# A pair's queries, keys and decays in three transfers at three places of the SyncE queue, instead of one

## The chip, the cores and the metric

One core of a Trainium2 chip runs the whole program. The metric is the device time of one execution in microseconds. Smaller is better.

## What is computed

A linear-attention layer with a decaying state is followed by two gated layers. The reference, cut down:

```python
# r, k, v, w: (4, 8, 768, 48); u: (8, 48)
for t in range(768):
    cur = einsum('bhd,bhe->bhde', u * k[t], v[t])
    y[t] = einsum('bhd,bhde->bhe', r[t], state + cur)
    state = w[t][..., None] * state + einsum('bhd,bhe->bhde', k[t], v[t])
x = y as (3072, 384)
x = (sigmoid(x @ w_gate) * (x @ w_val)) @ w_out          # 384 -> 1536 -> 384
h = x @ w_in                                             # 384 -> 2048
out = (h * tanh(softplus(h))) @ w_out2                   # 2048 -> 384
```

## The kernel before

**Stages.** Time is cut into 24 chunks of 32 steps, and two chunks make a *pair* (12 pairs, NP). For a pair, the queries, keys and decays (r, k, w, called R, K and W in the code) of 32 rows lie in one tile `blk` of 128 partitions and 10,240 bytes each; there are two such tiles, `blk[p % 2]`. For pair p the kernel does:

- `load_pair(p)`: fill `blk`. Pair 0 comes in three transfers (R, K, W), all others in one of 1,280 KB.
- `fine(p)`: GpSimd (POOL) multiplies queries by keys into `pt` tiles and folds decays into R, K and W in place (`update`, L455 for all of them); VectorE (DVE) sums each `pt` into the matrix `A` (L476). The first two products need R and K alone; every `update` of R or K needs W too.
- `coarse(p)` and `keys(p)`: DVE transposes K, R, W and A into `KD`, `RD`, `WD` and `X` (L566, L560, L573, L611); TensorE (PE) multiplies them (`lp`, L595); POOL and DVE scale them; K is updated twice more and transposed into `KT` (L654). That last transpose frees `blk[p % 2]` for pair p+2.
- `step(j)`, twice: outputs `yp` (L680), then the state `s` is decayed (L756), key-value products `kp` (L783) are made and added (`join`, L794). The outputs are split into two fp16 halves (`xs`, L207) and transposed by a DMA from the ScalarE queue into `xt` (L714).
- `gate(p, f)`, f from 0 to 11: 18 matmuls for gate and value (L828), then ScalarE and DVE make `gt`. `out1(p, c, part)`: output sums of the first gated layer (L892), three column groups c of four parts; after the fourth, `xo` is made and **stored to HBM** in `x2d` (L928).
- The second gated layer (L1013, L1058) follows at the end and reads `x2d` back.

`v` comes in its own transfers (`load_v`, four of 96 KB for a chunk), weights in raw tiles of 768 KB that are decoded on the chip.

**Order.** The program adds tasks with costs and dependences to a `Plan`; `Plan.run` computes due times backwards and lets each engine take the ready task with the earliest due time. What comes out is a fixed instruction order for each engine, in which the chip then runs it. All loads and stores named above are issued by SyncE (SP), one after another: an issue that waits holds all behind it. In the main loop over p (L1180), `gate(p, f)` and `out1(p-1, ...)` are added for f = 0 to 11, `tail1(p+1)` (coarse, keys and first step of the next pair) at f = 4, and `tail2(p+1)` (second step, `load_pair(p+3)`) and `fine(p+2)` at f = 7. On PE one turn of this loop, called *turn p* here, is 24 groups of nine gate matmuls, 12 groups of nine output sums, and between them, from f = 4 on, the many small matmuls of `lp`, `yp` and `kp`. From the last step's `kp` of a turn to f = 4 of the next there are none of these.

```python
        keys = [("blk", p % 2, i) for i in range(3)]
        if p:
            attn("sp", 3.6, lambda e: go(e, None), [], keys, lat=2.0)
```

Of the kernel before, what the change touches and what calls it, by code (L numbers as in the profile page):

```python
# [25 lines left out]
KC = DM // 128  # L26
# [29 lines left out]
class Plan:  # L56
# [11 lines left out]
    def add(self, eng, cost, fn, reads=(), writes=(), lat=SEM, burst=False):  # L68
        t = Task()
        t.cost = eng if isinstance(eng, dict) else {eng: cost}  # L70
        t.fn, t.lat, t.burst = fn, lat, burst
        t.rank = len(self.tasks)
        t.deps = set()
        for k in reads:
            if k in self.writer:
                t.deps.add(self.writer[k])
        for k in writes:
            if k in self.writer:
                t.deps.add(self.writer[k])
            t.deps.update(self.readers.pop(k, ()))  # L80
        for k in reads:
            self.readers.setdefault(k, []).append(t)
        for k in writes:
            self.writer[k] = t
        self.tasks.append(t)
# [66 lines left out]
def mixer_moe_kernel(  # L152
# [32 lines left out]
    x2d = dram.tile([NP, KC, 128, 2, NT], F16, name="x2d")  # L185
# [11 lines left out]
    def attn(eng, cost, fn, reads=(), writes=(), lat=SEM, burst=False):  # L197
        add(eng, cost, fn, [*reads, "attention"], writes, lat, burst)

    def split(key, src, hi, lo, scale, cost, reads, new):  # L200

        def high(e):
            new()
            nc.scalar.activation(out=hi(), in_=src(), func=AF.Copy, scale=scale)

        def rest(e):
            nc.vector.scalar_tensor_tensor(  # L207
                out=lo(), in0=src(), scalar=scale, in1=hi(), op0=ALU.mult, op1=ALU.subtract
            )

        add("act", cost, high, reads, [(*key, 0)])
        add("dve", cost, rest, [*reads, (*key, 0)], [(*key, 1)])
# [185 lines left out]
    kd = {}  # L398
    wd = {}
    lps = {}  # L400
    yps = {}
    kps = {}
    xss = {}
# [10 lines left out]
    def load_pair(p):  # L414
        edges = (0, C * DH, C * (DH + DP), BLK)

        def new(e):
            blk[p] = fp.tile([128, BLK], F32, tag=f"blk{p % 2}", name=f"blk{p}")

        def go(e, i):  # L420
            if i is None:
                new(e)
            cs = slice(0, BLK) if i is None else slice(edges[i], edges[i + 1])
            nc.sync.dma_start(out=blk[p][:, cs], in_=rkw[p, :, cs])

        keys = [("blk", p % 2, i) for i in range(3)]
        if p:
            attn("sp", 3.6, lambda e: go(e, None), [], keys, lat=2.0)
        else:
            attn("none", 0, new, [], keys, lat=0.0)  # L430
            for i in range(3):
                attn("sp", 1.2, lambda e, i=i: go(e, i), [], [keys[i]], lat=2.0)

    def load_v(j):
        def go(e):
# [444 lines left out]
    def out1(p, c, part):  # L880
        last = p == NP - 1
        bank = "po2" if last and c == 1 else "po"
        cs = slice(128 * c, 128 * c + 128)
        fr = range(3 * part, 3 * part + 3)

        def sums(e):
            if part == 0:
                pool = w2["po"] if bank == "po2" else po
                ops[p, c] = pool.tile([128, 512], F32, tag="po", name=f"o1{p}_{c}")
            for f in fr:  # L890
                for n, (a, g) in enumerate(((0, 0), (1, 0), (0, 1))):
                    nc.tensor.matmul(  # L892
                        ops[p, c][:, :NT],
                        wos[:, a, f, cs],
                        gt[p][:, g, f, :],
                        start=(f == 0 and n == 0),
                        stop=(f == NF1 - 1 and n == 2),
                    )

        reads = [("gt", p % 2, f, a) for f in fr for a in range(2)]  # L900
        reads.append(("gt", p % 2, "tile"))
        reads += [("wo", f // 2, a) for f in fr for a in range(2)]
        if bank == "po2":
            reads.append("open")
        add("pe", 0.99, sums, [*reads, "outs"], [bank])
        if part < 3:
            return
        n = nxo[0]
        nxo[0] += 1
        xo = ("xo", n % 3)  # L910

        def new():
            xos[n] = mp.tile([128, 2, NT], F16, tag=f"xo{n % 3}", name="xo")

        split(
            xo,
            lambda: ops[p, c][:, :NT],
            lambda: xos[n][:, 0],
            lambda: xos[n][:, 1],
            SX / (SW * SG),  # L920
            0.35,
            [bank],
            new,
        )
        add(
            "sp",
            0.4,
            lambda e: nc.sync.dma_start(out=x2d[p, c], in_=xos[n]),  # L928
            [(*xo, 0), (*xo, 1)],
            [("x2d", p, c)],  # L930
            lat=2.0,
        )
# [43 lines left out]
    def load_x2(r):  # L976
        def go(e):
            x2[r] = w2["p"].tile([128, 2, KC, NR], F16, tag=f"x2{r % 2}", name=f"x2_{r}")
            for i in range(2):
                for h in range(2):  # L980
                    nc.sync.dma_start(
                        out=x2[r][:, h, :, NT * i : NT * i + NT],
                        in_=x2d[2 * r + i, :, :, h].rearrange("c p n -> p c n"),
                    )

        src = [("x2d", 2 * r + i, c) for i in range(2) for c in range(KC)]
        add("sp", 2.4, go, [*src, "open"], [("x2", r % 2)], lat=2.0)
# [139 lines left out]
    attn("pool", 0.4, unit, [], ["eye"])  # L1127
    attn("sp", 0.1, lambda e: nc.sync.dma_start(out=U, in_=ub), [], ["U"], lat=2.0)
    load_pair(0)
    load_pair(1)  # L1130
    for j in range(3):
        load_v(j)
# [13 lines left out]
    def tail1(p):  # L1146
        coarse(p, cells[p])
        keys(p)
        step(2 * p)

    def tail2(p):
        step(2 * p + 1)
        if p + 2 < NP:
            load_pair(p + 2)

    def tail_end():
        done = [("blk", i, n) for i in range(2) for n in range(3)]
        done += [("pt", i) for i in range(5)] + [("A", i) for i in range(8)] + ["A"]
        add("none", 0, open_a, [], [*done, "opened"])
        for i in range(8):  # L1160
            cs = slice(256 * i, 256 * i + 256)
            dst = lambda cs=cs: w2["wi"][:, :, :, cs]
            load_raw(("wi", i), lambda: dp, in_cols(wi, cs), (KC, 256), i % 3)
            decode(("wi", i), dst, (KC, 256), i, i % 3, ["opened"], W2HI, W2LO)
        add("none", 0, open_b, [], ["attention", "open"])
        for i in range(8):
            cs = slice(2 * i, 2 * i + 2)
            dst = lambda cs=cs: w2["wp"][:, :, cs]
            slot = (i + 2) % (3 + NRAW)
            pool = (lambda: dp) if slot < 3 else (lambda: w2["raw"])  # L1170
            reads = [] if slot < 3 else ["open"]
            load_raw(("wp", i), pool, in_rows(wo2, cs), (2, DM), slot, reads)
            decode(("wp", i), dst, (2, DM), i, slot, ["open"], W2HI, W2LO)
# [6 lines left out]
    for p in range(NP):  # L1180
        for f in range(NF1):
            if p + 1 < NP:
                if f == YPOS[0]:
                    tail1(p + 1)
                if f == YPOS[1]:
                    tail2(p + 1)
                    if p + 2 < NP:
                        cells[p + 2] = fine(p + 2)
                    else:
                        tail_end()  # L1190
            if f == 0 and p >= NP - 1:
                load_x2(0)
                load_x2(1)
            gate(p, f)
            if p > 0:
                out1(p - 1, f // 4, f % 4)
    add("none", 0, lambda e: None, [], ["gates", "free_g"])
    add(
        "act",
# [61 lines left out]
```

## Time and profile before

| | |
|---|---|
| runs | 1020.68, 1025.45 and 1024.71 us; median 1024.71 us |
| profiled execution | 1025.36 us; its span, first to last instruction, 1023.6 us |
| busy share of the span | PE 92%, DVE 50%, ScalarE 34%, POOL 30% |
| mean granted TensorE clock | 0.988 of full speed |
| HBM traffic | 56.64 MB read, 9.44 MB written |

The profile names for each stretch in which an engine stands idle what ended it: another engine's instruction, a DMA, or "issue", if the engine waited for nothing that the profile shows. `PEld` are the weight loads of the PE, which overlap its matmuls. Queue q1 carries the DMAs that SP issues, q10 those of ScalarE, and q8 the instructions. Times within the trace are in microseconds from the first instruction.

### The profile page before, as it was taken

The page shows a single profiled execution, that of the slowest core. Times are in us where ns is not written, and L with a number is a line of the kernel's source. Part 1 is how long each engine was busy: PE and PEld are TensorE (multiplying, and loading weights), DVE is VectorE, ACT ScalarE, POOL GpSimd, SP SyncE. Part 2 cuts the span into 40 slices and gives each one's busy share as a digit, 9 for nine tenths or more (in the row PEclk, how much of TensorE's full clock was granted, in tenths as well). Part 3 has the DMA queues.
Part 4 walks back from the last instruction along what each step waited for, and adds up shares of the span by engine and source line. Part 5 has one row for each costly group of instructions (what it writes and reads, how often), then busy time and mean ns, then how long its engine had stood idle before and what let it go on. Part 6 is the DMA issues. An engine that isn't in the chain of part 4 may idle for free.

```text
span 1023.6 us, 32777 instructions
## 1 busy us (share of the span) xinstructions
PE 941.2 (92%) x14952; PEld 678.8 (66%) x14952; DVE 512.9 (50%) x831; ACT 347.1 (34%) x693; POOL 307.6 (30%) x322
## 2 busy tenths in 40 slices
PE   0388789989999899989999999999999999999998
PEld 0266678868878687878888887655555555555555
DVE  5899988866666556666658557221111111111110
ACT  3347622212212122222226356433333333333320
POOL 8873589671744444454113011000000000000000
PEclk9999899989999899999999999999999999999999
DMA  9345543222140404040206351010100101000000
GB/s 303 125 168 177 198 95 110 45 100 91 33 91 29 90 28 90 29 100 20 60 9 173 107 175 42 11 37 16 41 14 16 39 16 47 9 16 16 8 16 31
DMA packets 53595, 72.12 MB, mean 70 GB/s; under 512 B 20432, under 2 KB 37328, under 8 KB 52048
## 3 DMA queue, kind: packets, MB, share of 16 engines
q1 hardware_dynamic: 36816, 66.09, 21.2%
q10 hardware_dynamic: 16640, 3.94, 2.4%
q8 instruction: 117, 1.92, 0.8%
q14 instruction: 22, 0.18, 0.1%
HBM read 56.64 MB, written 9.44 MB: 65 GB/s over the span
## 4 chain that ended last, share of the span: by engine, by line
PE 78%; DVE 9%; DMA 4%; issue 3%; POOL 2%; ACT 2%; ACTq 0%; SPq 0%; DVEq 0%
PE gv L828 22%; PE o L1058 18%; PE h L1013 18%; PE o L892 11%; PE yp L680 3%; PE kp L783 3%; PE lp L595 3%; DMA raw_wo<-wo 1%; POOL pt L455 1%; DVE A L476 1%; POOL blk L455 1%; DVE word_wi L286 1%; DMA raw_wp<-wo 1%; DMA raw_wv<-wv 1%; DVE X L611 1%
## 5 line engine op out<-in xcount | busy, mean ns | idle before, releaser
L1013 PE MATMUL h<-x,wis 128*128 128x512 f16 x864 | 201.5, 379 | 0.0
L828 PE MATMUL gv<-xt,wgs 128*128 128x256 f16 x1296 | 167.4, 277 | 11.7 <-DVE gt L859 5.7
L828 PE MATMUL gv<-xt,wvs 128*128 128x256 f16 x1296 | 168.1, 276 | 4.3 <-issue 4.3
L892 PE MATMUL o<-gt,wos 128*128 128x256 f16 x1296 | 167.5, 275 | 4.4 <-DVE xo L207 1.9
L455 POOL TENSOR_TENSOR blk<-blk 128x384 f32<-128x384 f32 (+1 forms) x144 | 125.9, 890 | 70.0 <-DVE KD L566 59.3
L828 PEld LDWEIGHTS <-wgs 128*128 128x128 f16 x1296 | 124.9, 99 | 30.5 <-issue 12.6
L1013 PEld LDWEIGHTS <-wis 128*128 128x128 f16 x864 | 84.5, 98 | 90.7
L892 PEld LDWEIGHTS <-wos 128*128 128x128 f16 x1296 | 127.2, 98 | 24.2 <-issue 4.8
L828 PEld LDWEIGHTS <-wvs 128*128 128x128 f16 x1296 | 121.9, 99 | 23.4 <-issue 4.6
L839 ACT ACTIVATE sig<-gv 128x256 f32<-128x256 f32 x144 | 55.0, 383 | 236.4 <-PE gv L828 225.2
L1024 ACT ACTIVATE e<-h 128x512 f32<-128x512 f32 x96 | 57.3, 597 | 207.5 <-PE h L1013 207.5
L455 POOL TENSOR_TENSOR pt<-blk 128x384 f32<-128x384 f32 (+1 forms) x96 | 108.4, 1154 | 51.4 <-DMA blk<-rkw 47.3
L844 DVE SCALAR_TENSOR_TENSOR gv<-gv,sig 128x256 f32<-128x256 f32 x144 | 61.7, 429 | 82.7 <-ACT sig L839 82.2
L856 ACT CAST gt<-gv 128x256 f16<-128x256 f32 x144 | 53.2, 371 | 76.1 <-DVE gv L844 69.1
L859 DVE TENSOR_TENSOR gt<-gv,gt 128x256 f16<-128x256 f32 x144 | 60.3, 419 | 32.2 <-ACT gt L856 32.1
L595 PE MATMUL lp<-RD,KD 64*16 64x16 f32 (+1 forms) x3072 | 34.5, 185 | 37.0 <-DVE RD L560 33.6
L1031 DVE SCALAR_TENSOR_TENSOR wos<-e,wos 128x512 f16<-128x512 f32 x27 | 18.7, 692 | 84.5 <-ACT wos L1027 84.5
L595 PEld LDWEIGHTS lp<-RD,KD 64*16 64x16 f32 (+1 forms) x3072 | 29.8, 101 | 46.1 <-DVE RD L560 33.6
L1058 PE MATMUL o<-wps,wgs 128*128 128x384 f16 x324 | 58.5, 326 | 0.0
L1058 PE MATMUL o<-wps,wos 128*128 128x384 f16 x324 | 57.2, 326 | 0.0
L1031 DVE SCALAR_TENSOR_TENSOR wgs<-e,wgs 128x512 f16<-128x512 f32 x27 | 18.7, 692 | 73.8 <-ACT wgs L1027 73.8
L783 PE MATMUL kp<-v,KT 32*32 32x48 f32 x2944 | 45.9, 212 | 8.6 <-issue 7.5
(92 smaller groups left out, 1051.0 us busy)
## 6 DMA issues: line engine op xcount, KB each, us to landing
blk<-rkw SPq DMA_DIRECT2D x11, 1280.0 KB, 6.7
v<-vt SPq DMA_DIRECT2D x96, 96.0 KB, 3.3
raw_wi<-wi SPq DMA_DIRECT2D x8, 768.0 KB, 4.9
raw_wp<-wo SPq DMA_DIRECT2D x8, 768.0 KB, 4.4
raw_wg<-wg SPq DMA_DIRECT2D x6, 768.0 KB, 4.5
raw_wv<-wv SPq DMA_DIRECT2D x6, 768.0 KB, 4.8
raw_wo<-wo SPq DMA_DIRECT2D x6, 768.0 KB, 4.4
x2d<-xo SPq DMA_DIRECT2D x36, 128.0 KB, 1.8
```

Source lines behind the costliest of these rows:

```text
L455: engines[e].tensor_tensor(out=pv, in0=a, in1=b, op=ALU.mult)
L595: nc.tensor.matmul(out, kd[p][gs, x, :m], rhs, start=True, stop=True, skip_group_check=True)
L783: nc.tensor.matmul(kps[j, hf][o : o + 32, i, :], KT[o : o + 32, p % 2, HG * e + x, :], vs[j][o : o + 32, x, :], start=True, stop=True,)
L828: nc.tensor.matmul(gps[p, f][:, o], w[:, a, kc, fs], xt[p][:, c, kc, :], start=(n == 0), stop=(n == 3 * KC - 1),)
L839: nc.scalar.activation(out=sgs[p, f], in_=gps[p, f][:, 0], func=AF.Sigmoid, scale=1.0 / (SW * SX))
L844: nc.vector.scalar_tensor_tensor(out=gps[p, f][:, 1], in0=gps[p, f][:, 1], scalar=SG / (SW * SX), in1=sgs.pop((p, f)), op0=ALU.mult, op1=A ...
L856: nc.scalar.copy(out=gt[p][:, 0, f], in_=gps[p, f][:, 1])
L859: nc.vector.tensor_tensor(out=gt[p][:, 1, f], in0=gps[p, f][:, 1], in1=gt[p][:, 0, f], op=ALU.subtract,)
L892: nc.tensor.matmul(ops[p, c][:, :NT], wos[:, a, f, cs], gt[p][:, g, f, :], start=(f == 0 and n == 0), stop=(f == NF1 - 1 and n == 2),)
L1013: nc.tensor.matmul(hps[r, f], w2["wi"][:, a, kc, fs], x2[r][:, c, kc, :], start=(n == 0), stop=(n == 3 * KC - 1),)
L1024: nc.scalar.activation(out=es[r, f], in_=hps[r, f], func=AF.Mish, scale=ih)
L1058: nc.tensor.matmul(ops2[r, t][:, :DM], g2[r][f][:, c, tsl], w2["wp"][:, a, f, :], start=(f == 0 and n == 0), stop=(f == NF2 - 1 and n == 2),)
```

## The change

Pair 1 is still loaded at once. All other pairs are loaded in three transfers: R (384 KB), K (512 KB), W (384 KB). For pairs 2 and 3 the three are added together, where the one was. From pair 4 on only R is added there; K is added after the output sums of turn p-3, f = 11, with a planner's dependence on the store of `x2d[p-4]`, group 2, and W in turn p-2 after f = 3, with one on the store of `x2d[p-3]`, group 0. These dependences only set the order in the SP queue; the chip waits in front of them because the store, which waits for `xo`, is issued first.

```diff
         keys = [("blk", p % 2, i) for i in range(3)]
-        if p:
+        if p == 1:
             attn("sp", 3.6, lambda e: go(e, None), [], keys, lat=2.0)
-        else:
-            attn("none", 0, new, [], keys, lat=0.0)
-            for i in range(3):
-                attn("sp", 1.2, lambda e, i=i: go(e, i), [], [keys[i]], lat=2.0)
+            return
+
+        after = [[], [("x2d", p - 4, KC - 1)], [("x2d", p - 3, 0)]]
+        attn("none", 0, new, [], keys, lat=0.0)
+        for i in range(3):
+            late[p, i] = lambda i=i: attn(
+                "sp", 1.2, lambda e: go(e, i), after[i] if p > 3 else [], [keys[i]], lat=2.0
+            )
+            if p <= 3 or i == 0:
+                late.pop((p, i))()
...
+            if f == 3 and p > 1 and (p + 2, 2) in late:
+                late.pop((p + 2, 2))()
+            if f == 11 and (p + 3, 1) in late:
+                late.pop((p + 3, 1))()
```

The whole plan is made anew with it, so the order moves on every engine. On SP, one turn in the middle of the loop. Before, with the stores of `x2d[3]` group 0, 1, 2 and `x2d[4]` group 0 around the load of pair 8:

```order
L928 DMA x2d_86<-xo_4525 128x512
L424 DMA blk8_4932<-rkw 128x2560
L440 DMA v13_5032<-vt 32x768 x4
L928 DMA x2d_86<-xo_4905 128x512
L440 DMA v14_5235<-vt 32x768 x4
L928 DMA x2d_86<-xo_5265 128x512
L928 DMA x2d_86<-xo_5408 128x512
```

Now, with the stores of `x2d[3]` group 1 and 2 and of `x2d[4]` group 0 and 1:

```order
L935 DMA x2d_86<-xo_4868 128x512
L447 DMA v13_4949<-vt 32x768 x4
L447 DMA v14_5197<-vt 32x768 x4
L425 DMA blk8_5214<-rkw 128x768
L935 DMA x2d_86<-xo_5226 128x512
L425 DMA blk7_4342<-rkw 128x1024
L935 DMA x2d_86<-xo_5360 128x512
L425 DMA blk7_4342<-rkw 128x768
L935 DMA x2d_86<-xo_5753 128x512
```

The load of a pair no longer stands between the stores of group 0 and group 1; R of one pair and K of the pair before it stand around the store of group 2, and W stands behind the store of group 0.

On DVE, in the second half of turn 7 (`kp16_1` is the PE's last key product of chunk 16, `s17` the state that it is added to, which `yp17` needs). Before:

```order
L654 STREAM_TRANSPOSE KT_92<-blk9_5815 128x24x32
L207 SCALAR_TENSOR_TENSOR xs16_7566<-yp16_7461,xs16_7566 128x384
L207 SCALAR_TENSOR_TENSOR xo_7554<-o16_1_7226,xo_7554 128x256
L859 TENSOR_TENSOR gt7_7087<-gv7_7_7447,gt7_7087 128x256
L794 TENSOR_TENSOR s17_6876<-kp16_1_7588,s17_6876 128x384
L756 TENSOR_TENSOR s18_7568<-s17_6876,WD8_5878 128x384
```

Now:

```order
L207 SCALAR_TENSOR_TENSOR xo_7523<-o16_1_7184,xo_7523 128x256
L483 TENSOR_REDUCE A_91<-pt_7474 128x2x4x4
L207 SCALAR_TENSOR_TENSOR xs16_7538<-yp16_7431,xs16_7538 128x384
L618 STREAM_TRANSPOSE X9_7556<-A_91 128x32x32
L801 TENSOR_TENSOR s17_6843<-kp16_1_7561,s17_6843 128x384
L573 STREAM_TRANSPOSE KD9_7623<-blk9_6112 128x32x32
L851 SCALAR_TENSOR_TENSOR gv7_8_7528<-gv7_8_7528,sig_7621 128x256
L567 STREAM_TRANSPOSE RD9_7679<-blk9_6112 128x32x32
```

The last sum into A for pair 9 and the transposes into X, KD and RD now stand together around that join; before, the X transpose that stood next was one of pair 10, later in the turn.

## Rows read from the trace of the kernel before

**Rows 1.** The page: busy time of each engine, and the queue of instructions (packets, MB, share).

```profile
PE 941.2 (92%) x14952; PEld 678.8 (66%) x14952; DVE 512.9 (50%) x831; ACT 347.1 (34%) x693; POOL 307.6 (30%) x322
...
q8 instruction: 117, 1.92, 0.8%
```

**Rows 2.** Waits of PE from 145 to 600 us: total us, times, longest.

```profile
PE gv L828 <- issue: 8.6, 2, 4.3
PE yp L680 <- issue: 3.8, 2, 2.7
PE o L892 <- issue: 1.8, 1, 1.8
...
PE gv L828 <- DVE gt L859: 1.3, 1, 1.3
PE kp L783 <- issue: 0.8, 2, 0.4
```

**Rows 3.** Busy time by stretch: length, engines (instructions), granted clock, DMA share, GB/s.

```profile
163.03:460.53 297.50, 281.50 (x6555) 238.44 (x6552) 192.67 (x322) 67.55 (x176) 155.34 (x163) 0.98 0.28 69
310.76:363.55 52.79, 48.52 (x1095) 40.59 (x1093) 29.77 (x52) 10.98 (x29) 22.57 (x25) 0.94 0.26 56
460.53:506.26 45.73, 45.73 (x1094) 39.15 (x1092) 29.49 (x52) 10.99 (x29) 13.72 (x17) 1.00 0.16 38
```

**Rows 4.** Timeline in turn 5: start, length, engine, line, what, idle before it.

```profile
340.86 0.34 SPq L424 DMA_DIRECT2D blk<-rkw  x1
...
353.31 1.86 PE L828 MATMUL gv<-xt,wgs 128*128 128x256 f16 x8 [4.27 <-issue]
```

**Rows 5.** DMA from 341 to 350 us: queues (packets, MB, share), issue (KB, landing).

```profile
q1 hardware_dynamic: 242, 1.53, 75.9%
q10 hardware_dynamic: 805, 0.20, 20.1%
...
blk<-rkw SPq DMA_DIRECT2D x1, 1280.0 KB, 7.7
```

**Rows 6.** DMA from 350 to 353 us: the queue of instructions.

```profile
q8 instruction: 1, 0.02, 2.9%
```

**Rows 7.** Busy time by stretch, right behind that wait of PE.

```profile
353.30:359.00 5.70, 5.69 (x84) 4.04 (x84) 0.00 (x0) 0.00 (x0) 3.00 (x4) 0.50 0.07 14
```

**Rows 8.** Busy time by stretch: one without small matmuls, one with many.

```profile
316.00:321.00 5.00, 5.00 (x48) 4.49 (x46) 2.53 (x5) 1.33 (x4) 3.83 (x5) 1.00 0.00 0
...
331.00:336.00 5.00, 5.00 (x162) 4.34 (x148) 4.15 (x5) 0.65 (x2) 0.86 (x1) 1.00 0.03 7
```

**Rows 9.** Timeline of SP: stores of output sums, groups 2 and 0, in turn 6.

```profile
364.61 11.15 SPq L928 DMA_DIRECT2D x2d<-xo  x2
```

**Rows 10.** Instructions that write v, from 490 to 500 us: durations ns, first and last start.

```profile
L440 SPq DMA_DIRECT2D v<-vt x4: 332/416/1391, 492.9 to 495.2; - x4
```

**Rows 11.** Busy time by stretch, while that v lands.

```profile
495.00:500.00 5.00, 5.00 (x160) 4.33 (x152) 2.92 (x5) 1.62 (x4) 0.00 (x0) 1.00 0.21 63
```

**Rows 12.** Groups of instructions by form: count, busy us, mean ns, idle before.

```profile
L611 DVE STREAM_TRANSPOSE X<-A 128x1024 f32<-128x1024 f32 x12 | 23.4, 1953 | 0.0
...
L794 DVE TENSOR_TENSOR s<-kp,s 128x384 f32<-128x384 f32 x44 | 23.9, 547 | 14.7 <-PE kp L783 14.1
```

**Rows 13.** Waits of PE from 60 to 163 us.

```profile
PE gv L828 <- DVE gt L859: 4.5, 3, 2.4
PE kp L783 <- issue: 2.9, 2, 1.5
```

**Rows 14.** Timeline of SP: the load of pair 4.

```profile
132.20 0.35 SPq L424 DMA_DIRECT2D blk<-rkw  x1
```

**Rows 15.** Waits of POOL, whole span: total us, times, longest.

```profile
POOL pt L455 <- DMA blk<-rkw: 47.3, 9, 11.5
```

**Rows 16.** DMA issues, whole span: count, KB each, median us to landing.

```profile
blk<-rkw SPq DMA_DIRECT2D x11, 1280.0 KB, 6.7
...
blk<-rkw SPq DMA_DIRECT2D x2, 384.0 KB, 4.1
```

More of the change, by code (lines that the diff above doesn't have):

```diff
@@ L400, in mixer_moe_kernel @@
     lps = {}
+    late = {}
     yps = {}
```

## The prediction

> **What bounds the kernel now.** I read the page first. PE is busy for 92% of the span [rows 1], and turn 8 has no idle PE at all [rows 3], so only what stops PE counts. Next came PE's waits. From 145 to 600 us other engines cause little; 15.0 us (8.6 + 3.8 + 1.8 + 0.8) are put down to "issue" [rows 2]: PE had what it needs and nothing to run. Third, the time by turns. Turn 8, with about the same matmuls, takes 45.73 us, turn 5 takes 52.79 [rows 3]. What differs is the load of a pair: turn 5 has one, turn 8 none (pair 11 was loaded before).
>
> Fourth, what happens around one such wait. In turn 5 SP issues the load of 1,280 KB at 340.86; PE stands for 4.27 us and goes on at 353.31 [rows 4]. From 341 to 350 us the window's DMA answer lists two queues alone, q1 and q10, together 96% of the 16 engines; there is no packet of q8, the queue of instructions [rows 5]. From 350 to 353 there is one [rows 6]. PE and PEld run 2 x 14952 instructions and q8 brings 117 packets of some 16 KB [rows 1], so a packet holds about 256 of them if nearly all are PE's. Where the small matmuls are, PE starts 162 + 148 = 310 instructions in 5 us, without them 48 + 46 = 94 [rows 8]. So a late packet hurts only among the small matmuls: 256 instructions are 4.1 us there (256 / 310 x 5) and 13.6 us elsewhere. I read the wait as: **PE's next instructions come late because the long load of a pair fills the DMA engines in the dense half of a turn.** [...]
>
> **The change part by part.** *Where the transfers go.* In the new SP order, R of one pair stands behind both v of the turn, the second of which waits for the turn's last `kp`; then the store of group 2, then K. All that lies in the stretch with 94 instructions in 5 us, where 13.6 us go by for each 256. W stands behind the store of group 0. The two stores' issues run from 364.61 to 375.76 [rows 9], and turn 6 begins at 363.55 [rows 3], so W is issued about 12.2 us into the turn, where `lp` begins, and it is 384 KB.
>
> *Gain.* Turns 2 to 7 take 297.50 us [rows 3]. At turn 8's pace they take 6 x 45.73 = 274.4, which is 23.1 less. The other way to count: issue waits 15.0, and a clock of 0.98 over 297.5 us [rows 3], 6 us; together 21. Loads from pair 5 on and most of pair 4's leave the dense halves, so I take the middle: **-22 us**, with 15 (waits alone) and 23.1 as ends.
>
> *W among the small matmuls.* Its own price is not shown. Upper end: the smaller of the two issue waits of `yp`, 3.8 - 2.7 = 1.1 us [rows 2], for each of pairs 4 to 11: 8.8 us. Lower end 0: a v, four transfers of 96 KB and so the same 384 KB, is issued from 492.9 to 495.2 [rows 10] in the dense half, and PE is busy for all of the next 5.00 us with 160 matmuls [rows 11]. That is the nearest row, so I take **0**.
>
> *Two more issues and two more landings for a pair.* An issue holds SP for 0.34 us [rows 4]; SP has 11 us between stores [rows 9]. A transfer of 384 KB lands after 4.1 us where the whole lands after 6.7 [rows 16], so the parts take longer in sum. Who waits is POOL: it already waits 47.3 us in nine waits for pairs to land [rows 15], and PE doesn't wait for it in these turns [rows 2]. The cover is that a pair is loaded about two turns before its `lp`. The change spends most of it: W comes in turn p-2 at 12 us, and `lp` follows at the same place of turn p-1, 46 us later. POOL's work for a turn (13.7 to 22.6 us) and DVE's (about 30) [rows 3] must fit in there. **0**; without cover see the rivals.
>
> *The state's join.* POOL's products now end in the middle of the turn, so DVE's X transpose (1.95 us) stands directly before the join of `kp` to the state (0.55 us) [rows 12], for which `yp` waits. Between that `kp` and `yp` PE has 18 gate matmuls, 1.9 us at 48 in 5 us [rows 8]. If the transpose starts just as `kp` ends, PE waits 1.95 + 0.55 - 1.9 = 0.6 us; if it starts earlier, not at all. Ends 0 and, with the whole transpose late, 1.95 us in each of eight turns, 15.6. The natural place is between 0 and 0.6: 0.25 x 8 = **+2 us**.
>
> *The start.* Up to turn 1 DVE and the weights decide, and the plan has other orders there. PE's wait for issue before `kp`, 1.5 us at most [rows 13], falls beside the load of pair 4 at 132.20 [rows 14], whose K and W now come later: **-1.5**. PE's 4.5 us of waits for `gt` [rows 13] may go or come twice: ends -4.5 and +4.5.
>
> *The end.* Pair 11 is finished later, its W being held back into turn 9, and with it begins the decoding of the second layer's weights, still some turn and a half before its first matmul. That burst costs 1.3 us in a wait for `gt` [rows 2]; it may be paid twice. **+0.5**, ends 0 and 1.3.
>
> **Sum**: -22 + 0 + 0 + 2 - 1.5 + 0.5 = -21. The profiled execution took 1025.36 us: 1.76 outside its span of 1023.6, which the change leaves alone. 1025.36 - 21 = 1004.4. It lies 0.65 above the median of the runs shown, within their spread of 4.8.
>
> **The rivals.** *Chain too short, slower.* W is now late by plan, and all of a pair's POOL and DVE work hangs on it, in order: products, A, X, the join, `yp`. Each microsecond that the last product is later than I count makes `yp` wait one microsecond in eight turns. At 21 / 8 = 2.6 us a turn the gain is gone. [...] For it: W lands about when POOL needs it. Against: PE never waits for POOL there now, and POOL has half of each turn free. [...] 5%.
>
> *A late packet has another cause, no change.* If the instruction queue takes turns with the others, a packet waits for one packet of data and not for a load, and cutting the load leaves the waits where they are: the gain term is 0, and 1025.36 + 2 - 1.5 + 0.5 = 1026. For it: loads of one size go with waits from 0.4 to 4.3 us [rows 2]. Against: no packet of q8 in 9 us beside two full queues [rows 5]. [...] 6%.
>
> *Half.* W, or the heap of v, R, store and K (384 + 384 + 128 + 512 = 1,408 KB, more than the old load) that spills past its sparse stretch, still starves PE: 1.1 to 2.7 us [rows 2] a turn, 9 to 22 us of eight turns given back without the clock, so 1013 to 1026, likeliest 1014. 10%.
>
> **How the numbers follow.** Forecast 79%, half 10%, no change 6%, slower 5%. The forecast's own ends: 1025.36 - 23.1 - 4.5 = 998 with nothing lost, and 1025.36 - 15 + 1 = 1011 with the waits alone. To leave no more than 2 in 10 out the range goes on to the likely part of "half": 998 to 1015. About 0.5% (5 us) is what a measurement of this kernel can tell from no change: faster than 1019.6 takes the forecast and most of "half", 88%; within it 7%; slower 5%.
>
> **What would show it.** Right: issue waits of PE between 145 and 550 us under 3 us in all; no stretch at 0.50 of the clock there; turns 2 to 7 at 45.7 to 46.5 us each; in a turn's dense half only W and one v. The join term: waits of `yp` for DVE's `s`, under 0.6 us each. Wrong: issue waits just behind W's issue; PE waiting for X or `s` for microseconds; turns over 48 us; or a new slow-clock stretch in the first 160 us, which the new order there could cause as well as remove.

## The result, and the profile after

The changed kernel takes **1007.54 us** (median of four runs, 1006.19 to 1010.17), the kernel before in the same session 1022.69 (four runs, 1018.63 to 1025.45): a ratio of 0.9856, 95% interval 0.982 to 0.9891. Forecast were 1004.4, between 998 and 1015. The profiled execution of after took 1010.17 us with a span of 1008.4; it is the slowest of the four. Line numbers of after are 7 higher than before's from `load_v` on (`gv` L835, `lp` L602, `yp` L687, `kp` L790).

The page of after: PE's busy time, the granted clock in 40 slices, the queue of instructions. They answer to [rows 1].

```profile
PE 937.8 (93%) x14952; PEld 678.7 (67%) x14952; DVE 521.2 (52%) x830; ACT 345.9 (34%) x692; POOL 309.8 (31%) x324
...
PEclk9998889999999999999999999999999999999999
...
q8 instruction: 117, 1.92, 0.8%
```

The same instructions come in the same 117 packets, and PE is busy 3.4 us less. So the span, 15.2 us shorter, shrank mostly in PE's idle time. PE's waits in after from 145 to 600 us (total us, times, longest), to be laid beside [rows 2]:

```profile
PE o L899 <- DVE xo L207: 2.4, 2, 1.7
PE yp L687 <- DVE X L625: 1.3, 1, 1.3
PE yp L687 <- DVE s L801: 0.5, 1, 0.5
PE gv L835 <- DMA xt<-xs: 0.2, 1, 0.2
```

The word "issue", under which 15.0 us stood, is gone. The instruction packets come in time: in turn 5, from 30.2 to 39.2 us behind its start, before has none [rows 5], and after, in the same part of the turn (335.2 to 344.2 us), has two:

```profile
q8 instruction: 2, 0.03, 1.3%
```

Time by stretch in after (length, busy time of PE, PEld, DVE, ScalarE, POOL, clock, DMA share, GB/s): turn 0, turn 1, turns 2 to 8, and turn 10.

```profile
60.64:115.89 55.25, 44.02 (x1022) 35.44 (x1015) 48.99 (x88) 35.86 (x70) 25.17 (x25) 0.85 0.60 190
115.89:167.64 51.75, 45.90 (x1077) 39.75 (x1074) 46.33 (x69) 20.44 (x42) 35.33 (x35) 0.93 0.40 99
167.64:488.07 320.43, 320.40 (x7646) 274.14 (x7644) 215.23 (x360) 76.20 (x203) 156.01 (x167) 1.00 0.26 68
...
533.81:581.84 48.03, 44.55 (x966) 37.92 (x964) 36.40 (x53) 24.98 (x47) 16.24 (x9) 1.00 0.46 134
```

The same view of before, for the same turns:

```profile
60.92:109.90 48.98, 40.37 (x1138) 33.05 (x1134) 45.84 (x86) 33.34 (x67) 25.03 (x25) 0.97 0.61 198
109.90:163.03 53.13, 46.05 (x962) 38.38 (x956) 45.97 (x69) 20.77 (x41) 42.12 (x41) 0.94 0.47 124
163.03:506.26 343.23, 327.23 (x7646) 277.59 (x7644) 222.17 (x373) 78.54 (x205) 169.06 (x179) 0.98 0.26 64
553.46:598.29 44.83, 44.22 (x964) 37.79 (x965) 26.61 (x46) 18.80 (x41) 6.30 (x4) 1.00 0.35 108
```

In after PE is busy for 320.40 of the 320.43 us of turns 2 to 8, at full clock: seven turns of 45.73 to 45.93 us, turn 8's pace of before [rows 3] in each. Before took 343.23 for the same 7,646 matmuls. The balance of the two profiled executions: turns 2 to 8 **-22.8 us**; turns 0 and 1 together 107.0 for 102.1, **+4.9**; turn 9 -1.5; turn 10 +3.2; all behind it +1.25; what lies ahead of turn 0 -0.3. That is -15.2, the difference of the spans.

SP's queue in turn 4 of after (start, length of issuing):

```profile
259.91 0.36 SPq L425 DMA_DIRECT2D blk<-rkw  x1
260.37 0.37 SPq L935 DMA_DIRECT2D x2d<-xo  x1
260.80 0.42 SPq L425 DMA_DIRECT2D blk<-rkw  x1
271.18 0.33 SPq L935 DMA_DIRECT2D x2d<-xo  x1
271.56 0.43 SPq L425 DMA_DIRECT2D blk<-rkw  x1
```

R and K go out just behind the start of the turn (259.31), W follows 12.25 us into it. The prediction had worked out 12.2.

### The profile page after: what moved, and what is told of

It reads as the page before. It is cut to its first block, busy times and chain, and to the rows that moved or that the text cites. A ratio compares the mean times of both kernels' runs of the same rounds, so it can differ in the third digit from the quotient of the medians.

```text
span 1008.4 us, 32823 instructions
## 1 busy us (share of the span) xinstructions
PE 937.8 (93%) x14952; PEld 678.7 (67%) x14952; DVE 521.2 (52%) x830; ACT 345.9 (34%) x692; POOL 309.8 (31%) x324
## 4 chain that ended last, share of the span: by engine, by line
PE 81%; DVE 9%; DMA 5%; ACT 2%; issue 1%; ACTq 1%; SPq 0%; POOL 0%; DVEq 0%
PE gv L835 23%; PE o L1065 19%; PE h L1020 18%; PE o L899 12%; PE yp L687 3%; PE kp L790 3%; PE lp L602 2%; DMA raw_wv<-wv 2%; DMA raw_wg<-wg 1%; DVE A L483 1%; DVE word_wi L286 1%; DMA raw_wp<-wo 1%; DVE word_wi L275 1%; DMA raw_wo<-wo 1%; DVE X L618 1%
## 5 line engine op out<-in xcount | busy, mean ns | idle before, releaser
L835 PE MATMUL gv<-xt,wgs 128*128 128x256 f16 x1296 | 165.6, 275 | 4.3 <-DVE gt L866 3.7
L835 PE MATMUL gv<-xt,wvs 128*128 128x256 f16 x1296 | 166.3, 274 | 0.0
L462 POOL TENSOR_TENSOR blk<-blk 128x384 f32<-128x384 f32 (+1 forms) x144 | 128.8, 907 | 60.2 <-DVE WD L580 31.6
L835 PEld LDWEIGHTS <-wgs 128*128 128x128 f16 x1296 | 124.2, 98 | 22.0 <-issue 4.8
L835 PEld LDWEIGHTS <-wvs 128*128 128x128 f16 x1296 | 120.8, 98 | 17.9
L462 POOL TENSOR_TENSOR pt<-blk 128x384 f32<-128x384 f32 (+1 forms) x96 | 104.9, 1119 | 45.6 <-DMA blk<-rkw 44.1
L602 PE MATMUL lp<-RD,KD 64*16 64x16 f32 (+1 forms) x3072 | 34.9, 185 | 40.8 <-DVE RD L567 34.1
L602 PEld LDWEIGHTS lp<-RD,KD 64*16 64x16 f32 (+1 forms) x3072 | 30.1, 101 | 50.4 <-DVE RD L567 34.1
L483 DVE TENSOR_REDUCE A<-pt 128x32 f32<-128x768 f32 (+1 forms) x60 | 51.3, 862 | 0.8 <-POOL pt L462 0.8
```

Of the source, the lines that this page charges most:

```text
L462: engines[e].tensor_tensor(out=pv, in0=a, in1=b, op=ALU.mult)
L483: nc.vector.tensor_reduce(out=cell(), in_=shape(pts.pop(n)), op=ALU.add, axis=AX.X)
L602: nc.tensor.matmul(out, kd[p][gs, x, :m], rhs, start=True, stop=True, skip_group_check=True)
L835: nc.tensor.matmul(gps[p, f][:, o], w[:, a, kc, fs], xt[p][:, c, kc, :], start=(n == 0), stop=(n == 3 * KC - 1),)
```

## The experiments

The length of a turn says most, so here it is for some of the kernels, worked out from the start of each turn's first gate matmul; the last column is everything behind turn 10, up to the end of the span.

| kernel | turn 0 | 1 | 2 | 3 | 4 | 5 | 6 | 7 | 8 | 9 | 10 | rest |
|---|---|---|---|---|---|---|---|---|---|---|---|---|
| before | 49.0 | 53.1 | 55.6 | 44.4 | 47.7 | 52.8 | 48.3 | 48.7 | 45.7 | 47.2 | 44.8 | 425.3 |
| after | 55.2 | 51.7 | 45.9 | 45.7 | 45.7 | 45.7 | 45.8 | 45.7 | 45.7 | 45.7 | 48.0 | 426.6 |
| again | 57.5 | 50.7 | 46.0 | 45.7 | 45.7 | 45.7 | 45.7 | 45.7 | 45.7 | 45.7 | 47.9 | 424.7 |
| early_whole | 48.1 | 52.8 | 47.4 | 45.7 | 45.7 | 45.7 | 45.7 | 45.7 | 45.7 | 45.7 | 48.0 | 425.1 |
| cut_in_place | 50.3 | 54.1 | 48.2 | 46.1 | 48.5 | 49.0 | 47.9 | 47.3 | 45.7 | 47.0 | 45.1 | 426.0 |
| whole_moved | 55.4 | 51.4 | 48.3 | 44.6 | 47.0 | 45.8 | 46.8 | 47.2 | 47.1 | 50.6 | 45.7 | 425.2 |
| third | 49.1 | 54.2 | 48.7 | 46.1 | 45.8 | 45.7 | 45.7 | 45.7 | 45.7 | 47.4 | 44.4 | 425.9 |
| keys_alone | 49.0 | 53.8 | 50.0 | 45.7 | 47.2 | 46.8 | 46.2 | 45.9 | 45.7 | 47.4 | 44.3 | 427.1 |
| cut_in_ten | 52.8 | 56.3 | 48.5 | 44.9 | 47.3 | 46.0 | 45.9 | 46.2 | 45.7 | 45.9 | 46.0 | 425.5 |
| one_small | 52.1 | 53.4 | 50.4 | 45.4 | 49.9 | 49.6 | 49.4 | 49.4 | 45.7 | 46.3 | 45.6 | 426.9 |
| w_and_big | 55.9 | 50.8 | 45.7 | 46.0 | 47.3 | 47.4 | 45.7 | 45.7 | 45.7 | 46.2 | 47.8 | 425.2 |

The theory that was tested: PE's instruction packets come late beside a pair's load, because the load is long and stands among the small matmuls. Its parts are the **size** of the load, its **place** and the **cut** into several issues; the rival is a cause that has nothing to do with the load's length.

### First chip: cut alone, place alone, the start, the change again

**cut_in_place** keeps before's order on every engine and only issues each load as three transfers, back to back.

```diff
-            cs = slice(0, BLK) if i is None else slice(edges[i], edges[i + 1])
-            nc.sync.dma_start(out=blk[p][:, cs], in_=rkw[p, :, cs])
+            for n in range(3) if i is None and p > 1 else [i]:
+                cs = slice(0, BLK) if n is None else slice(edges[n], edges[n + 1])
+                nc.sync.dma_start(out=blk[p][:, cs], in_=rkw[p, :, cs])
```

> The kernel before with its own order on every engine; each load of a pair is issued as three transfers one right behind the other, at the old place. If PE's instructions come late because of how long the whole load keeps the DMA engines busy, nothing is won: issue waits of PE between 145 and 600 us stay at 11 to 19 us (15.0 before), the time at 1017 to 1026 us. If they come late because of the 10,240-byte packets of the one transfer (now 3,072 and 4,096), the waits fall below 4 us and the time to 1001 to 1008 us.

Measured: 1017.94 us beside 1023.81, ratio 0.9942 (0.991 to 0.9974). PE's waits from 145 to 600 us, those for issue:

```profile
PE gv L829 <- issue: 3.5, 2, 3.1
...
PE yp L681 <- issue: 2.0, 2, 1.3
PE kp L784 <- issue: 1.7, 2, 1.0
...
PE o L893 <- issue: 0.7, 1, 0.7
```

7.9 us in place of 15.0, in the same order and with the same bytes; that lies between the two outcomes that were expected. So the cut helps by itself, for some four tenths of the change's gain (0.6% of 1.4%).

**whole_moved** is the changed kernel, with every pair from 4 on in one transfer of 1,280 KB at K's new place.

```diff
+        if p > 3:
+            late[p, 1] = lambda: attn("sp", 3.6, lambda e: go(e, None), after[1], keys, lat=2.0)
+            return
         attn("none", 0, new, [], keys, lat=0.0)
```

> The changed kernel, but from pair 4 on the pair comes in one transfer of 1,280 KB again, placed where K is now, behind the store of output-sum group 2. If the place is what counts, there are no issue waits after 145 us, turns 2 to 8 take 45.7 to 46.0 us each, and the time is 1004 to 1011 us. If the cutting is needed too, one or two us of issue waits stay in each turn and the time is 1013 to 1022 us.

Measured: 1015.75, ratio 0.9926 (0.9895 to 0.9957). The two largest waits of PE from 145 to 600 us:

```profile
PE gv L838 <- DMA xt<-xs: 5.6, 5, 2.2
PE o L902 <- DVE xo L207: 2.7, 3, 1.4
```

Neither outcome came as it was expected. No issue wait is left, so the place does away with them even for a load of full size. But a new wait takes their place: the first gate matmuls of a turn wait for the output transposes `xt`, up to 2.2 us, and turns 4 to 9 take 284.4 us where after's take 274.5. The load itself is not in the way: around turn 6 the wait is at 352.3 and the load goes out at 355.9. The outputs are late: the last `xs` of turn 5 begins 5.8 us ahead of turn 6 (347.39), in after 7.6 us (343.17 before 350.78), and its transposes land after 4.6 us instead of 2.3. The plan is made anew for this kernel too, so this is the price of its order; a whole load at this place without that price was not tried. The nearest is k_and_more below, with 1,408 KB in two transfers there.

**early_whole** is the changed kernel with pairs 2 and 3 in one transfer, as before; in turns 0 and 1 PE's order is then before's.

```diff
-        if p == 1:
+        if 0 < p < 4:
```

> The changed kernel, with pairs 2 and 3 loaded in one transfer each as before; pairs 4 on are cut and late. Its order in turns 0 and 1 is that of the kernel before on PE. If the new order there costs the 6 us by which turn 0 grew (48.98 to 55.25 us), turn 0 is 48 to 51 us here, turn 1 51 to 53, and the time 1000 to 1005 us, 3 to 6 below the changed kernel. If the growth was the chance of one execution (the slow clock lasted 13.7 us there), the time is that of the changed kernel within 1.5 us.

**again** is the changed kernel once more, on this chip.

> The changed kernel once more, beside the others. If its order of the start is slow, turn 0 takes 53 to 56 us again; if the long slow-clock stretch was chance, 49 to 52. Time 1005 to 1010 us either way, and no issue waits of PE after 145 us.

Measured: early_whole 1006.18, ratio 0.982 (0.9792 to 0.9847); again 1008.87, ratio 0.9843 (0.9816 to 0.987). Turns 3 to 10 are alike to 0.1 us, but turns 0 and 1 take 100.9 in one and 108.3 in the other. Busy time by stretch, turn 0 of early_whole:

```profile
61.30:109.40 48.10, 40.45 (x1138) 32.99 (x1135) 46.06 (x85) 34.03 (x68) 24.26 (x25) 1.00 0.63 202
```

The clock is at 1.00 there; in again's turn 0 it is at 0.85, as in after's above. The intervals of the two kernels overlap, so that early_whole is the faster one is likely, not shown.

### Second chip: the size, and more bytes behind W and K

**third** has before's order and loads, from pair 4 on, only R (384 KB) at the old place; K and W are left out of it.

```diff
-            cs = slice(0, BLK) if i is None else slice(edges[i], edges[i + 1])
+            cs = slice(edges[i or 0], edges[(i or 0) + 1])
+            if i is None:
+                cs = slice(0, BLK if p < 4 else edges[1])
```

> The kernel before with its own order; from pair 4 on a load brings only R, 384 KB instead of 1,280, at the old place among the small matmuls (K and W are left out: the pair works on what was in the tile). If the length of the load is what holds PE's instructions up, issue waits between 145 and 600 us fall below 2 us and the time to 1000 to 1008 us. If any load at that place does it, the waits stay above 8 us and the time above 1015.

Measured: 1008.87 beside 1023.86, ratio 0.986 (0.9828 to 0.9893). No issue wait is left from 145 to 600 us, and turns 4 to 8 take 45.7 or 45.8 us; the time lies 0.9 us above the expected range. But the trace shows a hole in this run. R's part of the tile is free earlier than K's, and so from turn 4 on the load goes out some 12 us into the turn (316.87 in a turn 5 that begins at 304.5), and not some 30 us, as in before (340.86, from 310.76). Size and place changed together.

**keys_alone** closes that hole; it ran last, beside a before of 1025.35 us. It is third with K alone (512 KB) in place of R alone, since K's part is the last to come free. On every engine its order is before's.

```diff
-                cs = slice(0, BLK if p < 4 else edges[1])
+                cs = slice(0, BLK) if p < 4 else slice(edges[1], edges[2])
```

> Before's own order on every engine; each pair from 4 on loads only K (512 KB) at the old place of the queue, R and W are left out and the tile is filled again without them. It takes up a hole in the run third: there only R was loaded, whose part of the tile is free earlier, so in turns 4 to 7 its load went out some 12 us into the turn and not some 30 us, and size and place changed together. K's part is the last to come free, so this load should go out 29 to 37 us into turns 2 to 7, as before's does. If the size of the load makes the issue waits: under 3 us of them from 145 to 600 us, turns 4 to 7 at 45.7 to 46.5 us, 1007 to 1012 us. If the place alone makes them, and third was rid of them by its earlier start: 8 to 15 us of issue waits, single ones of 2 us and over, turns 4 to 7 at 47 to 50 us, 1017 to 1024 us.

Measured: 1007.67 us, ratio 0.9844 (0.9784 to 0.9904). In turn 5 the load goes out 30.0 us after the start, as in before. PE's waits for issue from 145 to 600 us:

```profile
PE gv L833 <- issue: 2.5, 2, 1.5
...
PE kp L788 <- issue: 0.2, 1, 0.2
```

Nothing has moved, only the load is shorter, and of the 15.0 us of issue waits 2.7 are left. So it is the load's size, at that place, that makes most of them. Turns 4 and 5, at 47.2 and 46.8 us, are above the expected 46.5.

**w_and_more** and **k_and_more** are the changed kernel with 896 KB copied from HBM to HBM behind each W (i = 2), or behind each K (i = 1), from pair 4 on. W and its copy are then 1,280 KB, the old load's size.

```diff
+            if i == 2 and p > 3:
+                nc.sync.dma_start(out=spare[p - 4], in_=rkw[p, :, :1792])
```

> The changed kernel with its own order; behind each W from pair 4 on SP also copies 896 KB of the same input to a scratch array in HBM, so that 1,280 KB are queued at W's place among the small matmuls (additional work that nothing reads). If length at that place counts, issue waits come back, 1 to 4 us a turn, 8 to 25 us in all, and the time is 1017 to 1032 us. If the cure was another (three transfers, order), the time stays at 1006 to 1011 us.

> The same 896 KB, but behind each K, where PE has large matmuls only. If a late packet of instructions hurts only among the small ones, no issue waits come and the time stays at 1006 to 1011 us, though 2,304 KB with v and R are queued there. If the amount counts wherever it stands, issue waits of 1 to 4 us a turn come here too, 1017 to 1032 us.

Measured: w_and_more 1010.44, ratio 0.987 (0.9841 to 0.99); k_and_more 1008.13, ratio 0.9854 (0.9823 to 0.9886). Waits for issue in w_and_more from 145 to 600 us:

```profile
PE lp L605 <- issue: 0.8, 1, 0.8
...
PE gv L838 <- issue: 0.8, 1, 0.8
PE o L902 <- issue: 0.6, 1, 0.6
PE kp L793 <- issue: 0.5, 1, 0.5
```

k_and_more is as expected from 145 to 550 us; its one issue wait, 0.7 us, is in turn 10, where again has 1.2 without a copy. w_and_more is a miss: 2.7 us of issue waits came back, 0.6 of them in turn 10, not the 15 of before. Length at a place where small matmuls begin is not enough.

**cut_in_ten** has before's order; each load from pair 4 on goes out as ten transfers of 128 KB, in one sequence at the old place.

```diff
+            cuts = edges[i : i + 2] if i is not None else (0, BLK)
+            if p > 3:
+                cuts = [256 * n for n in range(11)]
+            for a, b in zip(cuts, cuts[1:]):
+                nc.sync.dma_start(out=blk[p][:, a:b], in_=rkw[p, :, a:b])
```

> The kernel before with its own order; each load from pair 4 on is issued as ten transfers of 128 KB (1,024-byte packets) one right behind the other, at the old place. Three transfers there took some 6 us off and left 8 us of issue waits. If the size of a packet is a cause beside the length, ten take more off: waits below 5 us, 1005 to 1014 us. If what three won is that SP's issues spread the same load out a little, ten give the same within 3 us, 1014 to 1022 us.

Measured: 1014.56, ratio 0.9906 (0.9873 to 0.994); its turns 0 and 1 take 109.1 us, by 7.0 more than before's with the same order, 3.8 of them in turn 0, ahead of the first load in ten pieces (more on this start below). Its waits for issue from 145 to 600 us:

```profile
PE kp L786 <- issue: 0.4, 1, 0.4
PE yp L683 <- issue: 0.2, 1, 0.2
```

15.0 us have become 0.6, with every byte still at the old place. The waits are as expected if the size of a packet is a cause, the time is 0.6 us above that range and just inside the other.

### Third chip: size of packets or number of issues, and a yet longer W

Cutting into ten did two things: there are ten issues, and a row of the load is cut from 10,240 bytes into 1,024. **one_small** does the second alone: before's order, one issue, but the source is laid out so that the load comes in rows of 1,024 bytes.

```diff
+            if p > 3:
+                nc.sync.dma_start(
+                    out=blk[p].rearrange("q (c e) -> q c e", c=10),
+                    in_=rks[p].rearrange("c q e -> q c e"),
+                )
+                return
```

> The kernel before with its own order; from pair 4 on one transfer of the same 1,280 KB with one issue at the old place, but out of an array laid out so that it goes in packets of 1,024 bytes instead of 10,240. Ten transfers there left hardly any issue waits. If small packets did that (a packet of instructions waits behind a number of packets, not of bytes), the waits between 145 and 600 us are below 3 us here and the time 1004 to 1013 us. If the ten issues did it by feeding the load piece by piece, the waits stay at 8 to 19 us and the time at 1015 to 1026 us.

Measured: 1022.39 beside 1022.83, ratio 0.9989 (0.9958 to 1.002). The larger waits for issue from 145 to 600 us:

```profile
PE gv L835 <- issue: 4.0, 2, 2.1
PE yp L687 <- issue: 3.9, 2, 2.1
PE o L899 <- issue: 2.0, 1, 2.0
```

In all they are 10.2 us for 15.0 before. Single waits are shorter (2.1 at most where it was 4.3), but they are in five of the turns 2 to 7, and there is no gain. The two kernels side by side from 343.5 to 349.5 us, while the load of turn 5 is in the queue in both (it goes out at 342.35 in one_small and from 342.03 on in cut_in_ten): queues (packets, MB, share) in one_small,

```profile
q1 hardware_dynamic: 1400, 1.55, 86.2%
q10 hardware_dynamic: 832, 0.20, 18.8%
```

and in cut_in_ten:

```profile
q1 hardware_dynamic: 1266, 1.16, 74.1%
q10 hardware_dynamic: 832, 0.20, 15.7%
q8 instruction: 1, 0.02, 0.9%
```

Packets of the same kind (on q1 1.1 and 0.9 KB on average), but with one issue no instruction packet comes in 6 us and PE then stands for 2.08 us; with ten issues, spread over 5.62 us by SP, one comes in the middle of the load, and PE goes on. So with rows of one length it is the single issue that goes with the waits (10.2 us for 0.6); whether ten are rid of them because they are separate, or because they fill the engines less (74.1% for 86.2%), is not separated.

A single issue does not always go with such a wait, though. In turn 3 of before (218.59 to 263.02 us) PE has no wait for issue. Its load is issued at 249.37, 30.8 us behind the start, and DMA in before from 249.4 to 256.4 us, up to its landing, shows:

```profile
q8 instruction: 2, 0.03, 2.2%
...
blk<-rkw SPq DMA_DIRECT2D x1, 1280.0 KB, 6.9
```

Two instruction packets start before the whole load has landed. In this turn the output transposes and v are issued ahead of the load (from 245.61 and from 247.29 on); in turn 5 the transposes go out with it (340.76) and v behind it (343.14). That this makes the difference is not shown.

**w_and_big** is w_and_more with 1,216 KB for the copy, in rows of 9,728 bytes, so that W's place holds 1,600 KB.

```diff
-    spare = dram.tile([8, 128, 1792], F32, name="spare")
+    spare = dram.tile([8, 128, 2432], F32, name="spare")
```

> The changed kernel with its own order; behind each W from pair 4 on SP also copies 1,216 KB of the input to a scratch array in HBM, in rows of 9,728 bytes (896 KB in rows of 7,168 gave some 2 us of issue waits). If large packets among the small matmuls are enough, issue waits of 6 us or more come back in all and the time is 1012 to 1025 us. If it took the output transposes and v of the old place in the queue as well, the waits stay below 4 us and the time at 1007 to 1012 us.

Measured: 1010.41, ratio 0.987 (0.9818 to 0.9923). Waits for issue from 145 to 600 us, and the landing of the copy (count, KB, median us):

```profile
PE gv L838 <- issue: 1.6, 2, 1.4
PE lp L605 <- issue: 1.6, 1, 1.6
...
PE o L902 <- issue: 0.6, 1, 0.6
```

```profile
spare<-rkw SPq DMA_DIRECT2D x8, 1216.0 KB, 7.1
```

The copy lands after 7.1 us, like the load of before in turn 5 (7.7 [rows 5]), and yet there are only 3.8 us of issue waits, 3.0 of them in turns 4 and 5; the 0.6 us in turn 10 are not the copy's (again has 1.2 us there, without one). The old place had more beside the load: v, a store, and the output transposes, q10's 20.1% [rows 5]. Also the small matmuls are only beginning where W stands: in turn 4 of after, whose order it has, the first `lp` starts at 271.19 us, and W is issued at 271.56. And the copy ends in HBM, not in a tile. Which of these makes the rest of the 15 us stays open; no run here separates them.

**both** is early_whole with W of pair 11 right behind its K, some 10 us earlier than by the change (488.9 us in turn 9, where early_whole has 496.2, 1.9 and 12.2 us behind the turn's start).

```diff
+        if p == NP - 1:
+            after[2] = after[1]
...
+                if p + 3 == NP - 1:
+                    late.pop((p + 3, 2))()
```

> The changed kernel with pairs 2 and 3 in one transfer each, as in early_whole (1006.2 us), and W of the last pair loaded right behind its K, one turn earlier, so that the second layer's weights are decoded earlier. If the late end of the attention costs the 2 to 3 us that turns 9 to 11 grew, the time is 1002 to 1005 us. If PE's order of turn 10, which stays, costs them, it is 1005 to 1007 us.

Measured: 1007.19, ratio 0.9837 (0.9791 to 0.9883). Turn 10 takes 47.1 us where early_whole's takes 48.0, the rest 426.1 for 425.1; together 473.2 and 473.1. The time is 0.2 us above both expected ranges. Nothing is gained, so that W is late for pair 11 isn't what the end costs. Early_whole has the lowest median of all that was run, 1.4 us under that of after, 2.7 under again's on its own chip; these intervals can't tell that apart.

## Why the prediction was right

**The gain: right in size.** Turns 2 to 7 take 297.50 us in before [rows 3] and 274.7 in after (167.64 to 442.33), 22.8 less for a term of -22; turn 8 is unchanged. Both signs that were to show it are there: no issue wait from 145 to 550 us, and no granted clock under 1.00 in turns 2 to 8. One reservation: turn 2 of before is 55.6 us in this profile, and 50.4 in one_small, whose order and median are before's; so a single trace can be some us off here.

**Its reason: right in two parts, too simple in the third.** The load's size (keys_alone, 2.7 us for 15.0) and its place (whole_moved, none) each decide on the issue waits, and in after the clock of 0.50 behind them [rows 7] is gone with them. That a load as long would starve PE anywhere among small matmuls is contradicted by w_and_more and w_and_big, with 2.7 and 3.8 us of issue waits in all, and by a turn that the prediction didn't look at: turn 3 of before has a whole load in its dense half and no issue wait. So a long load there is needed for most of the waits, but it is not enough, and what else it takes stays open. And the prediction took "a load fills the engines" for one thing, where cut_in_ten shows that the same bytes at the same place cost 0.6 us when they are handed over in ten pieces. The rival "another cause, no change" fell with keys_alone. The prediction's own ground against it, no packet of q8 in 9 us [rows 5], is what one turn shows; in turn 3 two come in 7 us beside a whole load (above). In what way the queues take turns is not shown.

**W among the small matmuls: 0, right.** No issue wait stands behind W in after. Even with 1,216 KB more behind it the price is 3.8 us in all, under the upper end of 8.8.

**More issues and landings: 0, right.** POOL's waits for pairs to land, whole span, to be laid beside [rows 15]:

```profile
POOL pt L462 <- DMA blk<-rkw: 44.1, 10, 10.2
...
POOL blk L462 <- DMA blk<-rkw: 3.8, 5, 1.2
```

The second row, waits in front of the folds, is new. Together they are 47.9 us, about as long as before, and PE doesn't notice: the rival "chain too short" would show as waits of `yp` in eight turns, and between 167 and 534 us there is none.

**The join: +2 taken, 0 measured.** DVE's `X` does stand directly before the join, and takes 1.96 us as forecast, but PE waits for `s` once in the whole stretch, for 0.5 us, in turn 10. The transpose has begun early enough each time.

**The start: the step that failed in size.** Taken were -1.5 with ends of 4.5 to either side; measured +4.9. PE's first waits from 60 to 163 us in after, beside [rows 13]:

```profile
PE gv L835 <- DVE gt L866: 3.7, 3, 2.5
PE yp L687 <- DVE X L625: 3.2, 1, 3.2
PE lp L602 <- issue: 2.8, 2, 1.6
PE kp L790 <- issue: 2.2, 2, 1.5
```

The waits for issue did not go: in all they are 5.0 us for 3.1 (0.2 of these in front of `yp`): 2.2 in front of `kp` (2.9 before, one of them beside the load of pair 4, and that one is gone) and 2.8 in front of `lp`, where there were none. `yp` waits twice as long for `X` (3.2 for 1.6). More than these costs the clock. Busy time by stretch in after, from 75.0 to 78.3 us, then to 81.7, and from 95.4 to 109.1:

```profile
75.00:78.30 3.30, 1.09 (x59) 0.72 (x57) 2.69 (x7) 0.74 (x3) 1.80 (x3) 1.00 0.48 168
78.30:81.70 3.40, 2.81 (x83) 1.93 (x82) 2.06 (x5) 2.87 (x6) 0.00 (x0) 0.50 0.70 228
95.40:109.10 13.70, 10.91 (x272) 8.55 (x273) 11.27 (x17) 8.88 (x16) 3.57 (x4) 0.50 0.68 217
```

PE is busy for 1.09 of 3.30 us, and then the clock is at 0.50; in turn 0 of after it is there for 17.1 us, in before for 3.4, while turn 1 has 6.8 us of it in both. 10.91 us of busy PE at half the clock are some 5.5 us lost, by estimate. By the rows of both kernels PE is busy for 89.92 us in turns 0 and 1 together, where it was 86.42: so 3.5 of the +4.9 are a busy PE that takes longer, and 1.4 are idle time. The prediction named a new slow-clock stretch in the first 160 us as a thing that could go wrong, but gave it no price in the sum. How much of it is the order's and how much chance: turns 0 and 1 take 106.4 us on average in the six profiled kernels with after's order there (104.6 to 108.3) and 104.1 in the eight with before's (100.9 to 109.1). Turn 0 is longer with after's order (52.5 to 57.5 us for 48.1 to 52.8), turn 1 shorter (50.6 to 52.7 for 52.8 to 56.3). So the order is likely to cost some 2 us in all, and kernels with the same order there, though not with the same loads in turn 1, differ by more than that.

**The end: +0.5 taken, +3.0 measured.** In turn 10 PE waits 1.7 for `xo`, 1.3 for `X` and 0.5 for `s` (the first three rows of PE's waits above); before, it was 1.3 for `gt`. From turn 9 to the end, the seven kernels with after's order there and three loads to a pair take 519.1 us on average, the six with before's 518.0. So about +1 of the 3.0 is the order's, inside the ends of 0 and 1.3, and the rest is what two single traces differ by. Turn 10 itself is longer in every one of the seven (47.1 to 48.1 us for 44.3 to 46.0); turn 9 and what follows turn 10 give some two thirds of that back. What in the new order makes it is not settled; pair 11's late W is not it (both).

Against the sum of -21 the two profiled executions differ by -15.2: the start missed by 6.4, the end by 2.5, and the join, by -2, the gain, by -0.8, and what lies ahead of turn 0, by -0.3, gave some of that back. The start's +4.9 lies just outside its own end of +4.5; the time is inside the range because that was wide enough for it.

## What to carry to other kernels

Where PE stands with nothing to wait for in a dense run of small matmuls, look in that window for the packets of the instruction queue; if there are none beside a long transfer, try whether it helps to shorten the transfer (here 15.0 us of issue waits became 2.7, in keys_alone), to hand it over in several issues (0.6, in cut_in_ten), or to move it to a stretch in which PE starts fewer instructions (none, in whole_moved). Moving a load can exchange that wait for another (in whole_moved 5.6 us for the output transposes), so follow the work that the new order delays. And where a planner makes the whole order anew, price the stretches in which PE already waits: a sum worked out from a steady loop says nothing of them.

## What the runs showed of the hardware that was not expected

Handing over 1,280 KB in ten issues at the same place took the issue waits from 15.0 us to 0.6, while rows of 1,024 bytes in one issue left the time where it was (0.9989) and only shortened the longest wait, from 4.3 to 2.1 us. A transfer of 1,216 KB right behind W, 7.1 us long, made only some 3 us of issue waits at the start of the small matmuls, and in one turn of before a whole load among them made none. And with one and the same order of PE's instructions turn 0 took between 48.1 and 52.8 us in eight kernels; in the shortest (early_whole) the granted clock was 1.00 over the turn, in before, with 49.0 us, it was at 0.50 for 3.4 of them.
